# Where the operands of a chain of matmuls lie in SBUF, modulo 256 bytes

## The chip, the cores and the metric

The kernel runs on one core of one Trainium2 chip. The metric is the device time of one execution in microseconds (us), the median over several runs. Before the change it is 1124.74 us (three runs, 1123.02 to 1126.5).

## The reference

Four batches of twelve heads of attention over 448 positions (head size 64), with the scores capped by a tanh, feed two expert layers that all 1792 tokens go through:

```python
scores = cap * np.tanh(scale * np.matmul(q, k.transpose(0, 1, 3, 2)) / cap)
attn = softmax(scores)                                 # over the last axis
x = np.matmul(attn, v) ...                             # [1792, 768]
h = x @ w_in                                           # [768, 2048]
x = (h * np.cos(h)) @ w_out                            # [2048, 768]
a, b = x @ w1, x @ w2                                  # [768, 1024] each
out = ((a * b) @ w3) @ w_out2                          # [1024, 1024], [1024, 768]
```

The kernel computes w3 @ w_out2 first (called w2·w3 in what follows, after its tiles) and multiplies a * b by that product.

## The kernel before, in words

Every product is made of three matmuls in the type fp32r, since each operand is split into a high and a low part (tiles that end in h and l). The helper `mm3` issues them; its lines are 366, 367 and 368 of the profile:

```python
def mm3(out, wh, wl, xh, xl, first, last, on=False):
    PE.matmul(out, wh, xh, ...)   # L366: weights high, stream high
    PE.matmul(out, wh, xl, ...)   # L367: weights high, stream low
    PE.matmul(out, wl, xh, ...)   # L368: weights low, stream high
```

Each matmul loads its own 128x128 weights (a weight load, PEld) and then streams 448 columns (384 in w2·w3). So while L366 streams the high part, the weights of L367 are loaded; while L367 streams the low part, the weights of L368 are loaded; and while L368 streams the high part, the weights of the next L366 are loaded.

The program has four kinds of work. **Attention** (lines 577 to 605, 96 steps) streams the split queries qh, ql over the keys ks, and the probabilities p over v, in plain fp32 that takes several passes. Between its steps lie **w2·w3** (`make_w34`: stream w2, weights w3), and the start of **the first expert layer** (`moe1`: 384 calls of `mm3` with stream x and weights wi, 384 with stream g and weights wo). **The second expert layer** (`moe2`) is a Strassen-like scheme of seven products (`product`: 336 calls, stream y..., weights in the xh and xl tiles) followed by the output product (`o_unit`: 192 calls, stream ab, weights w34).

The order of all instructions is worked out when the kernel is built: each operation has a due time and a cost on each engine that may do it, and a planner (`Plan.schedule`) writes one list. On the chip each engine keeps that order and waits for the others through semaphores. The result of a unit of g is used by the matmuls two units later.

**Where the tiles lie.** `Ring` holds the buffers of one tile, `Pool` the pools. Pools of the left side begin where the one to the left ends; pools of the right side end at a fixed address and grow to the left. A tile lies behind the one created before it in its pool. A ring with `shift` gets 32 floats more and is read from `shift % PAD` floats on. `Ring.tile` gives the shifted view, `flat` the whole tile, and `seg` (L1087) cuts a segment of weights out of an x tile in the second expert layer. All chunks within a tile are multiples of 256 bytes apart where they are streamed, and of 512 where they are loaded as weights, so that each pair of tiles has one distance modulo 256. From the program before:

| stage | stream: address mod 256 | weights: address mod 256 |
|---|---|---|
| w2·w3 | w2h, w2l: 224 | w3h, w3l: 224 |
| first layer, into h | xh: 32, xl: 160 | wih, wil: 224 |
| first layer, out of g | gh, gl: 224 | woh, wol: 224 |
| second layer, products | y...h, y...l: 32 (yA22l: 160) | segments of xh: 96, of xl: 224 |
| second layer, output | abh: 32, abl: 160 | w34h, w34l: 224 |
| attention, scores | qh: 32, ql: 32 or 64 | ks: chunks at 32, 224, 160, 96 |

Of the kernel before, what the change touches and what calls it, by code (L numbers as in the profile page):

```python
# [10 lines left out]
F32 = mybir.dt.float32  # L11
F32R = mybir.dt.float32r
# [6 lines left out]
P = 128  # L19
B, H, S, D = 4, 12, 448, 64  # L20
CP = 112
NC = S // CP
DM = H * D
KD = DM // P
F1 = 2048
NF1 = F1 // P
F2 = 1024
# [5 lines left out]
INV2PI = 1.0 / (2.0 * math.pi)  # L33
CAP_MAX = 40.0
TWOPI = 6.283185
PAD = 32

# [3 lines left out]
class Ref:  # L43
    def __init__(self, item, sub=None, pick=None):
        self.item, self.sub, self.pick = item, sub, pick
# [25 lines left out]
class Ring:  # L71
# [7 lines left out]
    def tile(self, k):  # L79
        if not self.shift:  # L80
            return self.flat(k)
        t, n = self.flat(k), math.prod(self.shape[1:])
        t = t[:, self.shift % PAD:self.shift % PAD + n]
        return t if len(self.shape) == 2 else t.rearrange("p (a b) -> p a b", a=self.shape[1])

    def flat(self, k):
        if k not in self.tiles:
# [11 lines left out]


class Pool:
    def __init__(self, tc, name, **kw):
        self.tc, self.name, self.kw, self.rings, self.users = tc, name, kw, [], []

    def open(self):
        self.stack = ExitStack()
        self.pool = self.stack.enter_context(self.tc.tile_pool(name=self.name, bufs=1, **self.kw))

    def close(self):
        self.stack.close()  # L110


# [204 lines left out]
def program(  # L317
# [12 lines left out]
    general=False,  # L330
# [3 lines left out]
    G = dict(PAR, **GENERAL) if general else PAR  # L334
    plan = Plan()
# [38 lines left out]
    pools = {}  # L374

    def pool(name, **kw):
        pools[name] = Pool(tc, name, **kw)
        return pools[name]

    right = dict(side="right", reuse_waits="tile")  # L380
# [3 lines left out]
        pool(name, **kw)  # L384

    def ring(p, tag, shape, dtype=F32, n=2, shift=0):
        return Ring(plan, pools[p], tag, shape, dtype, n, shift)

    class Banks(Ring):
        def __init__(self, slots):  # L390
            Ring.__init__(self, plan, pools["psum"], "bank", [P, 512], F32, 0)
            self.free = [(0.0, k) for k in slots]
# [69 lines left out]
    ACT.activation(warm, warm, AF.Tanh)  # L462


    xh_r = ring("xring", "xh", [P, KD, S], F32R, 2, 0 if general else PAD)
    xl_r = ring("xring", "xl", [P, KD, S], F32R, 2, 0 if general else PAD)
    xh, xl = {}, {}
    A = {}
    tiles = [
# [380 lines left out]
    def pair(r):  # L850
        return r[0].ref(), r[1].ref()

    def hl(p, tag, shape, n, shift=0):
        return [ring(p, tag + t, shape, F32R, n, shift) for t in "hl"]
# [4 lines left out]
    def make_w34():  # L859

        raw_r, x_r = ring("wp", "raw", [P, 2 * DM], U32, G["nraw"]), ring("wp", "x", [P, DM], F32, G["nx"])
        w3_r = hl("wp", "w3", [P, F2 // 2], G["w3bufs"])
        w2_r = hl("wp", "w2", [P, DM], G["w2bufs"])
        sum_r = ring("wp", "sum", [P, DM], F32, NF2)
        NJ = NF2 // 2
        sums = [sum_r.new() for _ in range(NF2)]
        wo = {}
        runs = [(fc, p) for p in range(2) for fc in range(NF2)]
        need = {}
        for k, (fc, p) in enumerate(runs):  # L870
            need[fc, p] = G["wb"][p] + (G["we"][p] - G["wb"][p]) * fc / NF2
        for k, (fc, p) in enumerate(runs):
            due = need[fc, p]
            jcs = list(range(p * NJ, (p + 1) * NJ))

            new = {0: jcs, 3: [NJ], 6: [NJ + 1], NF2: jcs[2:]}.get(k, [])
            w3 = pair(w3_r)
            f64(due - G["e3"] * (k == 0), raw_r, x_r, w3T[fc, :, p * F2:(p + 1) * F2], F2 // 2, *w3)
            for n, jc in enumerate(new):
                wo[jc] = pair(w2_r)  # L880
                f64(due - (G["e2"] - n * G["e1"]) * (k == 0), raw_r, x_r, w_out2[jc], DM, *wo[jc])
            for n in range(2):
                half = slice(n * (DM // 2), (n + 1) * (DM // 2))
                acc = hy_r.ref()
                for q, jc in enumerate(jcs):
                    def f(acc=acc, q=q, jc=jc, half=half, w3=w3):
                        j = slice(q * P, (q + 1) * P)
                        mm3(acc()[:, :DM // 2], w3[0]()[:, j], w3[1]()[:, j], wo[jc][0]()[:, half],
                            wo[jc][1]()[:, half], q == 0, q == NJ - 1)

                    plan.op(due + n * 4 + q, [("PE", 3 * (DM / 4800 + 0.017), f)], r=[*w3, *wo[jc]], w=[acc])
                o = Ref(sums[fc], n, lambda t, half=half: t[:, half])
                a = acc[:, :DM // 2]
                if p == 0:
                    copy(due + n * 4 + 5, o, a, DM // 2, "AD", psum=True)
                else:
                    tt(due + n * 4 + 5, o, a, o, DM // 2, ALU.add, psum=True)
            if p == 1:
                z = w34_d.at(fc, lambda d, fc=fc: d[fc])
                o = Ref(sums[fc])  # L900
                dma(due + 12, z, o, r=[o], w=[z], kb=393, write=True)
        return raw_r, x_r
# [5 lines left out]
    def moe1(raw_r, x_r):  # L908
# [2 lines left out]
        wo_r = hl("mp", "wo", [P, DM], 4)  # L911
        hs_r, w_r = (ring("mp", t, [P, 2, S], F32, 2) for t in ("hs", "w"))
        kk_r = ring("mp", "kk", [P, S], F32, 1)
        g_r = hl("mp", "g", [P, 2, S], 2)
        y_r = ring("yp", "y", [P, KD, S], F32, 2)
        w_t, g_t, yacc = {}, {}, {}

# [26 lines left out]
        def chain(u, c, hp, due):  # L944

            if c == 0:
                g_t[u] = hs_r.new(), w_r.new()
            hs, w = (z.at(c, lambda t: t[:, c, :]) for z in g_t[u])
            copy(due, hs, hp, S, "AD", psum=True)
            plan.op(due + 1, [  # L950
                ("POOL", 0.16 + S / 1200,
                 lambda: POOL.tensor_scalar(w(), hs(), INV2PI, 0.25, op0=ALU.mult, op1=ALU.add)),
                ("DVE", 0.068 + S / 1920,
                 lambda: DVE.tensor_scalar(w(), hs(), INV2PI, 0.25, op0=ALU.mult, op1=ALU.add), True),
            ], r=[hs], w=[w])
            kk = kk_r.ref()
            plan.op(due + 2, [
                ("DVE", 0.068 + S / 1920,
                 lambda: DVE.tensor_scalar(kk(), w(), MAGIC, MAGIC, op0=ALU.add, op1=ALU.subtract), True),
            ], r=[w], w=[kk])  # L960
            tt(due + 3, w, w, kk, S, ALU.subtract, "PD")
            if c == 1:
                h2, w2 = (Ref(z) for z in g_t[u])
                plan.op(due + 5, [("ACT", 0.094 + 2 * S / 1200, lambda: ACT.activation(w2(), w2(), AF.Sin, scale=TWOPI))],  # L964
                        r=[w2], w=[w2], table="sin")
                tt(due + 6, w2, w2, h2, 2 * S, ALU.mult, "DP")
                g_t[u] = pair(g_r)
                copy(due + 7, g_t[u][0], w2, 2 * S, "APD")
                lo(due + 8, g_t[u][1], w2, g_t[u][0], 2 * S)

# [67 lines left out]
    def moe2():  # L1038
        raws = [ring("lp", "rawl", [P, 2 * DM], U32, 1), ring("q2", "rawq", [P, 2 * DM], U32, 1)]
        sts = [ring("lp", "stl", [P, DM], F32, 4), ring("q2", "stq", [P, DM], F32, 2)]  # L1040
        left_r = {x: hl("q2" if x == "A22" else "lp", f"y{x}", [P, KH, S], 1, PAD // 2 * (x == "A22")) for x in LEFT}
        w34_r, ab_r = hl("q2", "w34", [P, DM], 3), hl("q2", "ab", [P, S], 3, PAD // 2)
        c_r, tmp_r, ob_r = (ring("q2", t, [P, S], F32, n) for t, n in (("c", 11), ("tmp", 6), ("ob", 5)))
        V0, AB, OU = unit_due(4 * NP) + G["pu"], 63 * MM, 18 * MM
        left, right, cs = {}, {}, {}
# [39 lines left out]
                to("S4", a12, t + 5)  # L1085

        def seg(z, i, n):  # L1087
            if general:
                return z.tile().rearrange("p k s -> p (k s)")[:, i * HALF:(i + n) * HALF]
            return z.ring.flat(z.slot)[:, PAD // 2 + i * HALF:PAD // 2 + (i + n) * HALF]  # L1090

        def rights(p, fc, due):

# [79 lines left out]

        def o_unit(b, fc, due):

            w, ab = pair(w34_r), pair(ab_r)
            f32(due, sts[1], w34_d.at(fc, lambda d: d[fc]), DM, *w)
            halves(due - 1.5, ab, cs[b, fc], S)

            def one(m):  # L1180
                def go(at):
                    if fc == 0:
                        acc[m] = hy_r.ref()
                    o = acc[m]

                    def f():
                        mm3(o()[:, :S], w[0]()[:, m * P:(m + 1) * P], w[1]()[:, m * P:(m + 1) * P], ab[0](), ab[1](),
                            fc == 0, fc == NF2 - 1)

                    plan.op(at, [("PE", 3 * MM, f)], r=[*w, *ab], w=[o])  # L1190
                    if fc == NF2 - 1:
                        ob = ob_r.ref()
                        copy(at + 0.6, ob, o[:, :S], S, "AD" if m % 2 else "DA", psum=True)
                        dma(at + 1.5, Ref(out_i, (b, m)).view(lambda _: outT[b, m]), ob,
                            r=[ob], w=[Ref(out_i, (b, m))], kb=230, write=True)

                return go

            return [one(m) for m in range(KD)]
# [74 lines left out]
```

## Time and profile before

| | |
|---|---|
| median of three runs | 1124.74 us |
| time of the profiled execution | 1126.89 us |
| its span, first to last instruction | 1125.1 us |
| TensorE busy, matmuls (PE) | 1091.6 us, 97% |
| weight loads (PEld) | 941.1 us, 84% |
| VectorE (DVE) | 889.7 us, 79% |
| ScalarE (ACT) | 498.6 us, 44% |
| GpSimd (POOL) | 153.3 us, 14% |

PE is busy from the start of a matmul to its modelled end, and consecutive matmuls overlap; its busy share says that there was always one under way, not that the array ran at its peak. The weight loads run beside the matmuls. "L366" is a line of the kernel; helpers such as `mm3`, the copies (L342, L343) and the subtractions that make the low halves (L352) are called from many places, so the names of the tiles tell the stage.

### The profile page before, as it was taken

The numbers are of one execution on the slowest core, as the hardware profiler recorded it, in microseconds if no ns is written. First come the engines' busy times: TensorE is split into PE (matmuls) and PEld (weight loads), VectorE is DVE, ScalarE is ACT, GpSimd is POOL, SyncE is SP. The second block draws the span as 40 slices with busy tenths as digits, with TensorE's granted clock in tenths as the row PEclk, the third lists the DMA queues.
The fourth block names the chain that finished last, engine by engine and source line by source line (L and its number), as shares of the span: only waits on it lengthen the run. The fifth ranks groups of instructions, "written<-read, shape, count | busy, mean of one in ns | idle before, by whom it ended". The sixth has DMA issues, their size and how long they took to land. (4 is left out here: it accounts for less than half of the span.)

```text
span 1125.1 us, 13995 instructions
## 1 busy us (share of the span) xinstructions
PE 1091.6 (97%) x5040; PEld 941.1 (84%) x5040; DVE 889.7 (79%) x1353; ACT 498.6 (44%) x656; POOL 153.3 (14%) x145
## 2 busy tenths in 40 slices
PE   5899999999999999999999999999899999999997
PEld 3677777778888888889999999898789998999996
DVE  6888677799998989868789877777699879767642
ACT  4787667777655656541253211111244334221121
POOL 2222111112231111101001000000122200100000
PEclk9999999999999999999999999999899999999999
DMA  8885766877755655417633411104455435421132
GB/s 231 215 226 156 206 195 169 235 209 233 223 150 169 189 153 174 155 55 230 217 114 109 141 43 56 57 15 147 158 184 195 157 113 187 159 84 57 57 106 80
DMA packets 95554, 169.04 MB, mean 150 GB/s; under 512 B 37362, under 2 KB 68850, under 8 KB 95474
## 3 DMA queue, kind: packets, MB, share of 16 engines
q1 hardware_dynamic: 95474, 168.05, 49.7%
q8 instruction: 41, 0.67, 0.3%
q14 instruction: 39, 0.32, 0.1%
HBM read 129.30 MB, written 38.62 MB: 149 GB/s over the span
## 5 line engine op out<-in xcount | busy, mean ns | idle before, releaser
L605 PE MATMUL bank<-p,v 112*128 112x448 f32 x384 | 161.0, 542 | 0.0
L594 ACT ACTIVATE double<-double,ts 112x896 f32<-112x896 f32 x96 | 94.1, 981 | 76.9 <-PE double L585 76.7
L366 PE MATMUL bank<-xh,wih 128*128 128x448 f32 x270 | 108.3, 401 | 0.8 <-DVE xh L343 0.8
L605 PEld LDWEIGHTS bank<-p,v 112*128 112x128 f32 x384 | 72.8, 191 | 40.9 <-issue 38.0
L366 PE MATMUL bank<-gh,woh 128*128 128x448 f32 x260 | 102.3, 393 | 1.0 <-ACT hs L342 1.0
L367 PE MATMUL bank<-xl,wih 128*128 128x448 f32 x270 | 98.6, 365 | 0.2 <-DVE xl L352 0.2
L368 PE MATMUL bank<-xh,wil 128*128 128x448 f32 x270 | 98.4, 365 | 0.0
L594 ACT ACTIVATE p<-double,pac 112x896 f32<-112x896 f32 x96 | 96.9, 1011 | 2.4 <-PE bank L605 0.4
L367 PE MATMUL bank<-gl,woh 128*128 128x448 f32 x260 | 95.3, 367 | 0.0
L368 PE MATMUL bank<-gh,wol 128*128 128x448 f32 x260 | 95.1, 366 | 0.0
L352 DVE TENSOR_TENSOR y<-bank,y 128x448 f32<-128x448 f32 x111 | 68.5, 617 | 24.4 <-PE bank L368 24.0
L584 PE MATMUL double<-qh,ks 128*112 128x448 f32 x192 | 73.1, 381 | 13.7 <-DVE ks L352 9.7
L585 PE MATMUL double<-ql,ks 128*112 128x448 f32 x192 | 71.9, 375 | 0.0
L366 PEld LDWEIGHTS bank<-xh,wih 128*128 128x128 f32 x270 | 50.7, 188 | 10.2 <-issue 5.2
L366 PE MATMUL bank<-w2h,w3h 128*128 128x384 f32 x128 | 57.6, 450 | 1.7 <-ACT sum L342 1.7
L367 PEld LDWEIGHTS bank<-xl,wih 128*128 128x128 f32 x270 | 50.9, 188 | 9.3 <-issue 5.2
L819 POOL TENSOR_SCALAR wx<-rawc 128x768 f32<-128x768 f32 x29 | 34.7, 1195 | 168.0 <-DVE wil L352 65.8
L342 ACT COPY hs<-bank 128x448 f32<-128x448 f32 x39 | 20.8, 533 | 80.9 <-PE bank L368 80.9
L366 PEld LDWEIGHTS bank<-gh,woh 128*128 128x128 f32 x260 | 48.9, 188 | 8.7 <-issue 2.8
L367 PEld LDWEIGHTS bank<-gl,woh 128*128 128x128 f32 x260 | 49.0, 188 | 7.2 <-issue 3.5
L368 PEld LDWEIGHTS bank<-xh,wil 128*128 128x128 f32 x270 | 50.7, 188 | 3.9
L964 ACT ACTIVATE w<-w 128x896 f32<-128x896 f32 x32 | 30.5, 954 | 50.5 <-DVE w L352 50.4
(286 smaller groups left out, 2842.3 us busy)
## 6 DMA issues: line engine op xcount, KB each, us to landing
rawc<-in_w_out SPq DMA_DIRECT2D x16, 768.0 KB, 5.9
stq<-w_d SPq DMA_DIRECT2D x32, 384.0 KB, 3.4
qr<-in_q SPq DMA_DIRECT2D x48, 224.0 KB, 4.5
kr<-in_k SPq DMA_DIRECT2D x48, 224.0 KB, 4.8
rawc<-in_w_in SPq DMA_DIRECT2D x13, 768.0 KB, 4.9
raw<-in_w3T SPq DMA_DIRECT2D x16, 512.0 KB, 5.8
rawl<-in_w SPq DMA_DIRECT2D x9, 768.0 KB, 4.6
raw<-in_w_out SPq DMA_DIRECT2D x8, 768.0 KB, 6.9
```

The costliest lines, as they stand in the source:

```text
L342: "A": ("ACT", (0.051 if psum else 0.094) + n / 1200, lambda: ACT.copy(dst(), src())),
L352: "D": ("DVE", 0.068 + n / 960, lambda: DVE.tensor_tensor(dst(), a(), b(), op=op))
L366: PE.matmul(out, wh, xh, start=first, stop=False, skip_group_check=on)
L367: PE.matmul(out, wh, xl, start=False, stop=False, skip_group_check=on)
L368: PE.matmul(out, wl, xh, start=False, stop=last, skip_group_check=on)
L584: PE.matmul(o, w, qh(), start=True, stop=False)
L585: PE.matmul(o, w, ql(), start=False, stop=True)
L594: lambda f=f, x=x, o=o: ACT.activation(o(), s(), f, scale=x[:CP]))],
L605: PE.matmul(pv()[:, :S], w()[:, 2 * c + n].rearrange("p a d -> p (a d)"), p()[:, n, :], start=c == 0 and n == 0, stop=c == NT - 1 and n == 1)
L819: lambda: POOL.tensor_scalar(x(), h_().bitcast(F32), 0.0, 1.0, op0=ALU.mult, op1=ALU.mult)),
L964: plan.op(due + 5, [("ACT", 0.094 + 2 * S / 1200, lambda: ACT.activation(w2(), w2(), AF.Sin, scale=TWOPI))], r=[w2], w=[w2], table="sin")
```

## The change: addresses only

No instruction is added, removed or moved in the program; operands lie elsewhere. The padding of a shifted ring becomes 64 floats (256 bytes), and its view starts at `shift` floats (16 floats are 64 bytes, 48 are 192). The x rings lose their padding. w3 gets a shift of 48 floats; g becomes one tile with both halves and a shift of 16; ab becomes one tile with both halves and a shift of 16; yA22 keeps 16. The pool lp gets 16 floats at its front and the pool q2 gets 48 floats at its back. The weights' segments are now read from the start of the x tiles.

```diff
-PAD = 32
+PAD = 64
+PADS = {("lp", "front"): 16, ("q2", "back"): 48}
...
-        t = t[:, self.shift % PAD:self.shift % PAD + n]
-        return t if len(self.shape) == 2 else t.rearrange("p (a b) -> p a b", a=self.shape[1])
+        t = t[:, self.shift:self.shift + n]
...
+    def pad(self, end):
+        n = self.pads.get((self.name, end))
+        if n:
+            self.pool.tile([P, n], F32, name=f"{end}_{self.name}", bufs=1)
...
     def open(self):
...
+        self.pad("front")
 
     def close(self):
+        self.pad("back")
         self.stack.close()
...
-    xh_r = ring("xring", "xh", [P, KD, S], F32R, 2, 0 if general else PAD)
-    xl_r = ring("xring", "xl", [P, KD, S], F32R, 2, 0 if general else PAD)
+    xh_r = ring("xring", "xh", [P, KD, S], F32R, 2)
+    xl_r = ring("xring", "xl", [P, KD, S], F32R, 2)
...
-        w3_r = hl("wp", "w3", [P, F2 // 2], G["w3bufs"])
+        w3_r = hl("wp", "w3", [P, F2 // 2], G["w3bufs"], 48)
...
-        g_r = hl("mp", "g", [P, 2, S], 2)
+        g_r = ring("mp", "g", [P, 2, 2, S], F32R, 2, 16)
...
-                g_t[u] = pair(g_r)
+                g = g_r.new()
+                g_t[u] = [g.at(n, lambda t, n=n: t[:, n]) for n in range(2)]
...
-        left_r = {x: hl(..., [P, KH, S], 1, PAD // 2 * (x == "A22")) for x in LEFT}
-        w34_r, ab_r = hl("q2", "w34", [P, DM], 3), hl("q2", "ab", [P, S], 3, PAD // 2)
+        left_r = {x: hl(..., [P, KH, S], 1, 16 * (x == "A22")) for x in LEFT}
+        w34_r, ab_r = hl("q2", "w34", [P, DM], 3), ring("q2", "ab", [P, 2, S], F32R, 3, 16)
...
-            return z.ring.flat(z.slot)[:, PAD // 2 + i * HALF:PAD // 2 + (i + n) * HALF]
+            return z.tile().rearrange("p k s -> p (k s)")[:, i * HALF:(i + n) * HALF]
```

## Rows read from the trace of the kernel before

**Rows 1.** The page's part 1: busy us, share of the span, instructions

```profile
PE 1091.6 (97%) x5040; PEld 941.1 (84%) x5040; DVE 889.7 (79%) x1353; ACT 498.6 (44%) x656; POOL 153.3 (14%) x145
```

**Rows 2.** Busy time by stretch: PE, PEld, DVE, ACT, POOL; then clock, DMA share, GB/s

```profile
560.00:660.00 100.00, 100.00 (x491) 91.97 (x490) 89.38 (x147) 35.93 (x57) 10.35 (x9) 1.00 0.37 116
...
800.00:960.00 160.00, 153.09 (x735) 139.55 (x735) 144.36 (x224) 64.54 (x102) 22.33 (x16) 0.98 0.53 175
960.00:1125.10 165.10, 156.85 (x773) 144.60 (x772) 95.61 (x152) 32.58 (x55) 6.21 (x7) 0.99 0.27 85
```

**Rows 3.** What PE waited for: us in total, times, longest

```profile
PE bank L366 <- DVE yA22h L343: 2.8, 1, 2.8
PE bank L368 <- DVE w34l L352: 1.7, 1, 1.7
```

**Rows 4.** Timeline of PE in the first layer: start us, us, instruction

```profile
601.53 0.37 PE L366 MATMUL bank<-xh,wih 128*128 128x448 f32 x1
...
602.74 0.36 PE L366 MATMUL double<-gh,woh 128*128 128x448 f32 x1
...
603.97 0.36 PE L366 MATMUL bank<-xh,wih 128*128 128x448 f32 x1
```

**Rows 5.** Timeline of all engines near the end: a weight load beside a matmul

```profile
1115.19 0.36 PE L367 MATMUL bank<-abl,w34h 128*128 128x448 f32 x1
1115.19 0.19 PEld L368 LDWEIGHTS bank<-abh,w34l 128*128 128x128 f32 x1
```

**Rows 6.** Groups of PE in 500 to 795 us: count, busy us, mean ns

```profile
L366 PE MATMUL bank<-gh,woh 128*128 128x448 f32 x122 | 44.8, 367 | 0.0
...
L367 PE MATMUL bank<-gl,woh 128*128 128x448 f32 x122 | 44.8, 367 | 0.0
L368 PE MATMUL bank<-gh,wol 128*128 128x448 f32 x122 | 44.7, 366 | 0.0
...
L368 PE MATMUL bank<-xh,wil 128*128 128x448 f32 x108 | 39.4, 365 | 0.0
L367 PE MATMUL bank<-xl,wih 128*128 128x448 f32 x108 | 39.4, 364 | 0.0
L366 PE MATMUL bank<-xh,wih 128*128 128x448 f32 x108 | 39.4, 364 | 0.0
```

**Rows 7.** The same of PE in 960 to 1125 us, the second layer

```profile
L367 PE MATMUL bank<-abl,w34h 128*128 128x448 f32 x48 | 17.5, 366 | 0.0
...
L366 PE MATMUL bank<-abh,w34h 128*128 128x448 f32 x48 | 17.3, 360 | 0.0
...
L368 PE MATMUL bank<-yS2h,xl 128*128 128x448 f32 x12 | 4.4, 367 | 0.0
...
L366 PE MATMUL bank<-yA22h,xh 128*128 128x448 f32 x12 | 4.4, 366 | 0.0
L367 PE MATMUL double<-yA22l,xh 128*128 128x448 f32 x12 | 4.4, 366 | 0.0
...
L367 PE MATMUL bank<-yS2l,xh 128*128 128x448 f32 x12 | 4.4, 363 | 0.0
...
L366 PE MATMUL bank<-yS2h,xh 128*128 128x448 f32 x11 | 4.0, 363 | 0.0
```

**Rows 8.** The same of PE in 60 to 180 us, w2·w3

```profile
L367 PE MATMUL bank<-w2l,w3h 128*128 128x384 f32 x91 | 30.6, 336 | 0.0
```

**Rows 9.** Timeline of PE in one attention step, scores

```profile
146.03 0.36 PE L584 MATMUL double<-qh,ks 128*112 128x448 f32 x1
146.23 0.37 PE L585 MATMUL double<-ql,ks 128*112 128x448 f32 x1
146.44 0.37 PE L584 MATMUL double<-qh,ks 128*112 128x448 f32 x1
146.65 0.36 PE L585 MATMUL double<-ql,ks 128*112 128x448 f32 x1
```

**Rows 10.** Timeline of DVE at the start of the second layer

```profile
797.11 0.63 DVE L352 TENSOR_TENSOR tmp<-bank,tmp 128x448 f32<-128x448 f32 x1 [3.94 <-PE bank L368]
...
802.46 0.38 DVE L343 CAST yA22h<-stq 128x448 fp32r<-128x448 f32 x1
```

More of the change, by code (lines that the diff above doesn't have):

```diff
@@ L82, in tile @@
         t, n = self.flat(k), math.prod(self.shape[1:])
-        t = t[:, self.shift % PAD:self.shift % PAD + n]
-        return t if len(self.shape) == 2 else t.rearrange("p (a b) -> p a b", a=self.shape[1])
+        t = t[:, self.shift:self.shift + n]
+        if len(self.shape) == 2:
+            return t
+        if len(self.shape) == 3:
+            return t.rearrange("p (a b) -> p a b", a=self.shape[1])
+        return t.rearrange("p (a b c) -> p a b c", a=self.shape[1], b=self.shape[2])
     def flat(self, k):
@@ L101, with __init__ @@
 class Pool:
-    def __init__(self, tc, name, **kw):
-        self.tc, self.name, self.kw, self.rings, self.users = tc, name, kw, [], []
+    def __init__(self, tc, name, pads, **kw):
+        self.tc, self.name, self.pads, self.kw, self.rings, self.users = tc, name, pads, kw, [], []
+    def pad(self, end):
+        n = self.pads.get((self.name, end))
+        if n:
+            self.pool.tile([P, n], F32, name=f"{end}_{self.name}", bufs=1)
     def open(self):
@@ L376, in pool @@
     def pool(name, **kw):
-        pools[name] = Pool(tc, name, **kw)
+        pools[name] = Pool(tc, name, {} if general else PADS, **kw)
         return pools[name]
@@ L386, in ring @@
     def ring(p, tag, shape, dtype=F32, n=2, shift=0):
-        return Ring(plan, pools[p], tag, shape, dtype, n, shift)
+        return Ring(plan, pools[p], tag, shape, dtype, n, 0 if general else shift)
     class Banks(Ring):
@@ L1040, in moe2 @@
         sts = [ring("lp", "stl", [P, DM], F32, 4), ring("q2", "stq", [P, DM], F32, 2)]
-        left_r = {x: hl("q2" if x == "A22" else "lp", f"y{x}", [P, KH, S], 1, PAD // 2 * (x == "A22")) for x in LEFT}
-        w34_r, ab_r = hl("q2", "w34", [P, DM], 3), hl("q2", "ab", [P, S], 3, PAD // 2)
+        left_r = {x: hl("q2" if x == "A22" else "lp", f"y{x}", [P, KH, S], 1, 16 * (x == "A22")) for x in LEFT}
+        w34_r, ab_r = hl("q2", "w34", [P, DM], 3), ring("q2", "ab", [P, 2, S], F32R, 3, 16)
         c_r, tmp_r, ob_r = (ring("q2", t, [P, S], F32, n) for t, n in (("c", 11), ("tmp", 6), ("ob", 5)))
@@ L1087, in seg @@
         def seg(z, i, n):
-            if general:
-                return z.tile().rearrange("p k s -> p (k s)")[:, i * HALF:(i + n) * HALF]
-            return z.ring.flat(z.slot)[:, PAD // 2 + i * HALF:PAD // 2 + (i + n) * HALF]
+            return z.tile().rearrange("p k s -> p (k s)")[:, i * HALF:(i + n) * HALF]
         def rights(p, fc, due):
@@ L1174, in o_unit @@
         def o_unit(b, fc, due):
-            w, ab = pair(w34_r), pair(ab_r)
+            w, ab = pair(w34_r), ab_r.new()
+            ab = [ab.at(n, lambda t, n=n: t[:, n]) for n in range(2)]
             f32(due, sts[1], w34_d.at(fc, lambda d: d[fc]), DM, *w)
```

## The prediction

> **What bounds the kernel now.** I read the page's busy times first, then the stretches, the waits of TensorE, the timeline of a steady stage, and last the groups of matmuls with their mean durations. Matmuls are under way for 1091.6 of the 1125.1 us span [rows 1], and in the first layer for 100.00 of 100 us [rows 2]. What TensorE waits for after the start is a few single events of 1 to 3 us [rows 3]. The clock is granted in full in the first layer (1.00, the 2.4 GHz level), so no clock hides behind the busy time. The kernel goes at the pace of the matmul chain: 491 matmuls in 100 us are 204 ns from start to start, where 448 columns at 2.4 GHz are 187. Some 17 ns per matmul are not streaming.
>
> Is that remainder the same everywhere? In the timeline six matmuls of stream x take 1.21 us (601.53 to 602.74), and the next six, of stream g, take 1.23 (602.74 to 603.97) [rows 4]. Their form is the same; the tiles differ. A matmul's row says 0.36 us though the next one starts 0.20 us later: the modelled end adds about 0.16 us to every row, so differences between mean durations are differences of pace, and I work with these. In the first layer stream g has 366 to 367 ns, stream x 364 to 365 [rows 6]; in the second, the rows go from 360 to 367 [rows 7].
>
> What differs is where the operands lie. The weight load of the next matmul starts together with the stream of the present one and lies beside it (both at 1115.19, 0.19 us of it) [rows 5]. So the pair that may collide is a stream and the *following* load. From the table of addresses, its distance (stream minus next weights, modulo 256) is 0 for all of g; 64 for xh, 192 for xl; for y it is 192 behind L366 and L368 and 64 behind L367; for yA22 192 throughout; for ab 64 behind abh within a unit and 192 behind abl. Beside the rows: distance 0 has 366 to 367; distance 64 has 364 and 365 (xh), 363 (yS2l), 360 (abh, L366); distance 192 has everything: 363 (yS2h, L366), 364 (xl), 366 (abl, yA22h, yA22l), 367 (yS2h, L368). So 64 is low each time in matmuls with 128 columns of weights, 0 is high, and 192 is mixed.
>
> **The change part by part.** Addresses after it, worked out from the order of the tiles. The x tiles are 42 times 256 bytes without padding, so xh and xl all lie at 32; wi stays at 224. Both g tiles grow by 256 bytes: g lies at 224 + 64 = 32, wo at 224. w3 lies at 224 + 192 = 160 and w2 at 224. lp begins 64 bytes behind 32, so y lies at 96, and its weights, now at the start of the x tiles, at 32. q2 grows by 192 more than a multiple of 256 and ends where it did, so w34 moves to 32, ab and yA22 to 96. Attention moves as a whole by a multiple of 256. Every stream and following load in the two layers and in w2·w3 is then 64 apart; attention keeps its distances.
>
> What each part is worth in duration of matmuls (negative is gain):
> - g: 1152 matmuls go from distance 0 to 64. They should do as x does, whose streams lie at 32 over weights at 224 exactly as g then will: 366.7 to 364.3 on the mean of three rows [rows 6], -2.4 ns each, -2.8 us.
> - Products of the second layer, L368 (336): 367 at 192 to the 363 to 364 of yS2l at 64 [rows 7]: -3.5 ns, -1.2 us. L366, at 363 already, is taken at nothing.
> - yA22, L366 and L367 (96): 366 to 363: -0.3 us.
> - ab, L367 (192): 366 to 363: -0.6 us.
> - xl, L367 (384): 364 at 192, at most 1 ns to gain: -0.2 us, between 0 and -0.4.
> - w2·w3 (384): distance 0, and no row shows this shape elsewhere. Its row has 336 [rows 8], which less the 0.16 us is some 175 ns against 160 of streaming. The bounds: -0.9 us by the gain of g, +3.8 us if it goes the way of the attention row below (10 ns). I take -0.6, nearer to g, since it is the same three-line helper with 128 columns of weights.
>
> Sum: -5.7 us. Part of it is not kept: from 800 to 960 us VectorE is busy for 144.36 of 160 us [rows 2], and there TensorE waits for a low half that VectorE makes (w34l, 1.7 us) [rows 3]. If TensorE comes earlier, this wait grows. The gain in that stretch is about 1.5 us; I give back 0.4. The largest wait, 2.8 us for yA22h at the start of the second layer [rows 3], does not grow: VectorE's row before that chain had itself waited 3.94 us for a matmul [rows 10], so the chain starts earlier with TensorE. Net -5.3 us.
>
> What costs nothing: merging g's two halves, and ab's, in one tile adds no instruction. Both halves are freed by the same last matmul before and after. If a reader of the high half had now to wait for the low half, the matmuls concerned come two units later for g, which covers the VectorE subtraction; without that cover it is one wait of at most 1 us per unit, 32 units. New neighbours in reused memory can only add a wait for tiles whose last reader is long done at that point of the order.
>
> The profiled execution took 1126.89 us, 1.8 beyond its span and 2.2 above the median of the runs. From it, -5.3 gives 1121.6; from the median of 1124.74, which the time is compared with, **1119.4 us**.
>
> The Trainium skill speaks against any gain: "TensorE: Matmul & The Clock Gate", section "Step-by-step: what each phase is for", says that TensorE has two independent SBUF read ports, so that loading the next weights takes no read bandwidth from the running matmul. By that rule the sum would be 0, which is the first rival below; the trace bears it out for the overlap as such [rows 5], but rows of one form that differ by 7 ns [rows 7] speak against it in full.
>
> **The rivals.**
> 1. *Distance is not the cause.* What differs between tiles may be their order in the chain (L368 precedes a change of weights, g follows attention) or the traffic of other engines. For it: xl at 192 is as fast as xh at 64 [rows 6], and the same 192 gives 363 and 367 [rows 7]. Against it: g and x alternate in the same stretch with the same neighbours, and the low rows are at 64 three times. The change then does little: 0 to -3.4 us, 1121.4 to 1124.7, 1123.5 in the middle. Chance 0.24.
> 2. *The pace falls further.* abh reaches 360 at 64 [rows 7]. If all 3888 matmuls of the two layers came near that, 3 to 4 ns each below the mean of about 364.5, it is -8 to -15 us: 1110 to 1116. Against it: xh at 64 has 364 to 365 in over 200 rows [rows 6]. Chance 0.09.
> 3. *64 is the worse distance where weights or streams change shape.* In attention qh streams while the same chunk of ks is loaded once more; at distance 0 (146.03) the next start comes after 0.20 us, at distance 64 (146.44) after 0.21 [rows 9]. The order of the distances is turned round there. If that holds for w2·w3 (up to +3.8 us), and for the L366 of the products and for xl, which leave 192 (672 matmuls, up to +3 ns, +2.0), while g gains little (-0.5), the time is about 1130. It decides from the point where these lose more than g gains. Against it: ks has 112 columns of weights, and its chunks are 448 bytes apart. Chance 0.06.
>
> **How the numbers follow.** The forecast has 0.61, with -3.4 to -8 us. The likeliest is 1119.4. The range of 8 in 10 goes from 1114.0, well into rival 2, to 1124.0, which takes in most of rival 1; it leaves out the far end of rival 2 and all of rival 3. What a measurement of this kernel can tell from no change is about 0.3%, 3.4 us. Faster by more: forecast and rival 2, 0.70. Within: rival 1, 0.24. Slower: rival 3, 0.06.
>
> **What would show it.** In the profile after, the rows of stream g should read 364 to 365 instead of 366 to 367, and L368 of the products 363 to 364 instead of 367; abl and yA22 near 363; attention's rows unchanged. w2·w3 should read some 334 to 335. The stretch of the first layer without attention should be about 1% shorter per matmul for g's half. VectorE's, ScalarE's and GpSimd's rows and counts should stay, and the waits of rows 3 stay within half a us. If g's rows stay at 366 to 367 at the new distance, rival 1 holds and the prediction is wrong at its first step; if they fall but the time does not, it is the waits.

## The result, and the profile after

| | before | after |
|---|---|---|
| median of the runs compared | 1126.37 us (6) | 1115.24 us (6) |
| ratio, 95% interval | | 0.9906 [0.9887, 0.9925] |
| span of the profiled execution | 1125.1 us | 1114.7 us |

The change makes the kernel 0.94% faster, 10.6 us by the ratio (8.4 to 12.7 by its interval); the forecast was 5.3 us. The order of the instructions is the same on every engine; ScalarE and GpSimd have one semaphore wait more each. The lines of the profile are 12 higher than before: L366 to L368 of `mm3` are L378 to L380, L343 is L355, L352 is L364.

The page's busy times of the kernel after, to be read against [rows 1]:

```profile
PE 1078.9 (97%) x5040; PEld 937.4 (84%) x5040; DVE 885.6 (79%) x1353; ACT 498.4 (45%) x656; POOL 156.1 (14%) x145
```

Matmuls are under way for 12.7 us less (1091.6 to 1078.9), the span is shorter by 10.4: TensorE's idle time has grown by 2.3 us in this execution. The stretches, columns as in [rows 2]:

```profile
555.00:655.00 100.00, 99.88 (x500) 93.16 (x499) 89.66 (x148) 35.98 (x57) 10.70 (x9) 1.00 0.37 120
795.00:955.00 160.00, 154.10 (x754) 141.55 (x755) 144.60 (x224) 64.38 (x102) 22.52 (x16) 0.99 0.55 181
955.00:1114.70 159.70, 151.16 (x754) 140.70 (x752) 92.19 (x146) 31.53 (x53) 6.20 (x7) 0.98 0.24 80
```

In 100 us of the first layer stand 500 matmuls, where there were 491. That is 200 ns from one to the next instead of 204, at the same clock. The timeline, columns as in [rows 4]:

```profile
594.33 0.36 PE L378 MATMUL bank<-xh,wih 128*128 128x448 f32 x1
...
595.52 0.36 PE L378 MATMUL double<-g,woh 128*128 128x448 f32 x1
...
596.73 0.36 PE L378 MATMUL bank<-xh,wih 128*128 128x448 f32 x1
...
597.92 0.36 PE L378 MATMUL double<-g,woh 128*128 128x448 f32 x1
...
599.12 0.36 PE L378 MATMUL bank<-xh,wih 128*128 128x448 f32 x1
...
600.33 0.36 PE L378 MATMUL double<-g,woh 128*128 128x448 f32 x1
```

Six matmuls of x take 1.19 us, six of g 1.21, then x 1.19, g 1.20 and x 1.21. Both are faster, and what is left between them is scatter of single sixes. The groups of the first layer, 495 to 787 us, as in [rows 6]:

```profile
L380 PE MATMUL bank<-g,wol 128*128 128x448 f32 x122 | 44.2, 362 | 0.0
...
L379 PE MATMUL bank<-g,woh 128*128 128x448 f32 x122 | 44.1, 362 | 0.0
L378 PE MATMUL bank<-g,woh 128*128 128x448 f32 x122 | 44.1, 361 | 0.0
...
L380 PE MATMUL bank<-xh,wil 128*128 128x448 f32 x108 | 39.1, 362 | 0.0
L379 PE MATMUL bank<-xl,wih 128*128 128x448 f32 x108 | 39.1, 362 | 0.0
L378 PE MATMUL bank<-xh,wih 128*128 128x448 f32 x108 | 39.0, 361 | 0.0
```

g fell from 366 to 367 down to 361 to 362, further than x stood before; and x itself fell from 364 to 365 to 361 to 362, in all three lines. The second layer, 955 to 1115 us, as in [rows 7]:

```profile
L379 PE MATMUL bank<-ab,w34h 128*128 128x448 f32 x48 | 17.4, 362 | 0.0
L378 PE MATMUL bank<-ab,w34h 128*128 128x448 f32 x48 | 17.3, 360 | 0.0
...
L379 PE MATMUL double<-yA22l,xh 128*128 128x448 f32 x12 | 4.3, 362 | 0.0
...
L380 PE MATMUL double<-yS2h,xl 128*128 128x448 f32 x12 | 4.3, 362 | 0.0
L378 PE MATMUL bank<-yA22h,xh 128*128 128x448 f32 x12 | 4.3, 361 | 0.0
...
L380 PE MATMUL bank<-yS2h,xl 128*128 128x448 f32 x9 | 3.3, 363 | 0.0
L379 PE MATMUL bank<-yS2l,xh 128*128 128x448 f32 x9 | 3.3, 362 | 0.0
L378 PE MATMUL bank<-yS2h,xh 128*128 128x448 f32 x9 | 3.2, 360 | 0.0
```

Every row of [rows 6] and [rows 7] that stood at 366 or 367 is at 360 to 363. L366 of the products, forecast to stay at 363, came down to 360 as well. What TensorE waits for, as in [rows 3]:

```profile
PE bank L378 <- DVE yA22h L355: 2.8, 1, 2.8
PE bank L378 <- DVE xh L355: 2.2, 1, 2.2
PE bank L380 <- DVE w34l L364: 1.7, 1, 1.7
```

The two waits of [rows 3] are as long as they were. New in this size is the one for xh. In the timelines of TensorE, of the kernel before and then of the one after, it stands here:

```profile
223.89 0.37 PE L368 MATMUL bank<-xh,wil 128*128 128x448 f32 x1
225.06 0.47 PE L366 MATMUL bank<-xh,wih 128*128 128x448 f32 x1 [0.80 <-DVE xh L343]
```

```profile
221.32 0.36 PE L380 MATMUL bank<-xh,wil 128*128 128x448 f32 x1
223.91 0.49 PE L378 MATMUL bank<-xh,wih 128*128 128x448 f32 x1 [2.23 <-DVE xh L355]
```

TensorE arrives 2.57 us earlier, but leaves only 1.15 us earlier: VectorE, which makes xh there, is not on TensorE's pace. This is one execution: the profile of `abs0` below, whose matmuls go at the same pace, has no such wait.

### The profile page after: what moved, and what is told of

The parts are those of the page before. It is cut to its first block, busy times and chain, and to the rows that moved or that the text cites. A ratio compares the mean times of both kernels' runs of the same rounds, so it can differ in the third digit from the quotient of the medians.

```text
span 1114.7 us, 13997 instructions
## 1 busy us (share of the span) xinstructions
PE 1078.9 (97%) x5040; PEld 937.4 (84%) x5040; DVE 885.6 (79%) x1353; ACT 498.4 (45%) x656; POOL 156.1 (14%) x145
## 5 line engine op out<-in xcount | busy, mean ns | idle before, releaser
L378 PE MATMUL bank<-xh,wih 128*128 128x448 f32 x270 | 107.8, 399 | 2.7 <-DVE xh L355 2.2
L378 PE MATMUL bank<-g,woh 128*128 128x448 f32 x260 | 100.7, 387 | 0.0
L380 PE MATMUL bank<-xh,wil 128*128 128x448 f32 x270 | 98.0, 363 | 0.0
L380 PE MATMUL bank<-g,wol 128*128 128x448 f32 x260 | 94.2, 362 | 0.0
L379 PE MATMUL bank<-g,woh 128*128 128x448 f32 x260 | 94.1, 362 | 0.0
L364 DVE TENSOR_TENSOR y<-bank,y 128x448 f32<-128x448 f32 x111 | 68.5, 617 | 21.8 <-PE bank L380 21.3
L378 PEld LDWEIGHTS bank<-xh,wih 128*128 128x128 f32 x270 | 50.7, 188 | 11.7 <-issue 5.0
L378 PE MATMUL bank<-w2h,w3h 128*128 128x384 f32 x128 | 57.5, 449 | 0.0
L379 PEld LDWEIGHTS bank<-g,woh 128*128 128x128 f32 x260 | 48.8, 188 | 6.7 <-issue 3.5
L378 PEld LDWEIGHTS bank<-g,woh 128*128 128x128 f32 x260 | 48.8, 188 | 6.6 <-issue 2.8
L380 PEld LDWEIGHTS bank<-xh,wil 128*128 128x128 f32 x270 | 50.8, 188 | 3.4
```

The source lines that it names most:

```text
L364: "D": ("DVE", 0.068 + n / 960, lambda: DVE.tensor_tensor(dst(), a(), b(), op=op))
L378: PE.matmul(out, wh, xh, start=first, stop=False, skip_group_check=on)
L379: PE.matmul(out, wh, xl, start=False, stop=False, skip_group_check=on)
L380: PE.matmul(out, wl, xh, start=False, stop=last, skip_group_check=on)
```

## The experiments

A measure that needs less rounding than the rows: the mean time from the start of a matmul to the start of the next, from the start times of the trace, without matmuls next to attention's fp32 ones and without gaps over 230 ns. In what follows, g, x and so on "have" such a time. Before, g has 204.6 ns, x 202.4, products 202.7, yA22 203.7, ab 201.5 and w2·w3 174.9. After, all five streams of 448 columns have 200.0 to 200.1, w2·w3 173.3. Each comes from one profiled execution. Ratios of times are against the kernel before on the same chip.

**One part alone, and from the other side.** `g_alone` puts g 64 bytes further within its pool by two spacers, in the kernel before:

```diff
+SPACE = {("gh", 0): 16, ("woh", 2): 48}     # floats before that tile
...
+            n = self.plan_space.get((self.tag, k))
+            if n:
+                self.pool.pool.tile([P, n], F32, name=f"space_{self.tag}{k}", bufs=1)
```

> The kernel before with the first layer's g alone moved 64 bytes behind wo (g at 32, wo at 224 modulo 256; g stays two tiles, nothing else moves). Distance theory: g's rows fall from 366 to 367 ns to 361 to 362, and time by 1152 matmuls of about 4.5 ns, 5 us. The x rows stay at 364 to 365 if a matmul's pace hangs on its own distance alone; they fall to near 362 if x gained after the change because g, its neighbour in the stage, moved. If the gain came from merging g's halves in one tile or from the other moves: g's rows stay at 366 to 367, time within 1 us of before.

Time 0.9977 [0.9965, 0.9989]. Its groups in 500 to 785 us (L373 to L375 are `mm3`):

```profile
L374 PE MATMUL bank<-gl,woh 128*128 128x448 f32 x122 | 44.4, 364 | 0.0
L375 PE MATMUL bank<-gh,wol 128*128 128x448 f32 x122 | 44.2, 363 | 0.0
L373 PE MATMUL bank<-gh,woh 128*128 128x448 f32 x122 | 44.1, 361 | 0.0
L374 PE MATMUL bank<-xl,wih 128*128 128x448 f32 x108 | 39.6, 367 | 0.0
...
L373 PE MATMUL bank<-xh,wih 128*128 128x448 f32 x108 | 39.1, 362 | 0.0
```

g goes to 200.6 ns without being merged into one tile. The mean of x stays at 202.4, but is dealt out anew among its lines: L366 is 2 ns faster, L367 3 ns slower. A single line's row is therefore no measure of that line's distance; the mean over the three is. The time fell by 2.6 us, under the 4.6 that the pace gives; the ends of the interval are 1.2 and 3.9. No run shows where the rest went.

`wo_moved` has 16 floats more at the back of the pool, so g is back at 224 and wo at 160:

```diff
+SPACE = {("gh", 0): 16, ("woh", 2): 48}
+BACK = {"mp": 16}
```

> The same distance of 64 made from the other side: g stays at 224 modulo 256 and its weights wo move to 160. Distance theory: g's L366 and L367 fall to 361 to 362 ns as in the run with g moved; L368 before a load of wi (distance 0 there) keeps some of its loss; x before a load of wo is now at 128. Time 3 to 5 us under before. Theory that the absolute address of the stream counts (224 slow, 32 fast): g's rows stay at 366 to 367, time within 1 us of before.

g has 200.6 ns again, x 201.7, where `g_alone` left it at 202.4; the time is 0.9958 [0.9945, 0.9972]. Moving the weights does for g what moving the stream does: the distance counts, and not the stream's own address. L368 of g, which was expected to keep some of its loss, is the fastest of the three lines, 198.6 ns.

`x_alone` reads xl from 128 bytes further on:

```diff
-        t = t[:, self.shift % PAD:self.shift % PAD + n]
+        off = PAD if self.tag == "xl" else self.shift % PAD
+        t = t[:, off:off + n]
```

> The kernel before with xl alone read from 128 bytes further on in the first layer, so that it lies 64 and not 192 bytes behind the weights that are loaded beside it; xh, g and the second layer stay. In the profile after the change x gained 2.5 ns in all three lines though xh had kept its distance. If a matmul's pace hangs on the distances of its neighbours too (L367 at 64 helps L366 and L368): all three x lines fall from 364 to 365 to near 362, time by 1152 matmuls of 2 ns, 2.3 us. If each matmul counts by itself: L367 falls by at most 1 to 2 ns, L366 and L368 stay, time by 0.4 to 0.8 us. If x gained from g's move: nothing falls here.

x comes to 201.2 ns (200.9, 202.2 and 200.5 in its three lines, from 202.4, 202.6 and 202.3), g to 203.7; time 0.9983 [0.9973, 0.9993]. So L366 and L368, whose distances did not change, gained 1.5 and 1.8, and L367, whose distance did, 0.4. A matmul's pace hangs on its neighbours' distances too.

`first_layer` has both edits, g and xl.

> The kernel before with both edits of the first layer, g at 64 and xl at 64; second layer and w2w3 as before. Alone, g came to 600.6/3 = 200.6 ns with x unmoved at 202.4, and xl's move brought x to 201.2 with g near its old pace (203.7). If the two stages, which alternate every six matmuls, help each other: both near 200.1 as in the changed kernel, time 0.65% under before (2304 matmuls of 3.3 ns, 7.6 us), more than the two runs alone (0.23 and 0.17%) add up to. If they merely add: g 200.6 and x 201.2, time 0.45% under before. The second layer's rows must stay at those of before.

g has 200.2 and x 200.1 ns; in the second layer the products have 202.8 and ab 201.4, as before. The time is 0.9937 [0.9913, 0.9960]. Alone, g gained 4.0 ns, which left x where it was, and x 1.2, with 0.9 for g beside it; together they gain 4.4 and 2.3. A part of the gain of x comes only when both move. In time that is 7.1 us against 2.6 and 1.9 for the parts, with intervals of 1 to 3 us on each.

**The distance swept.** In the changed kernel all distances are set to one value by the paddings; here for 32, the others alike:

```diff
-PADS = {("lp", "front"): 16, ("q2", "back"): 48}
+PADS = {("xring", "front"): 56, ("lp", "front"): 8, ("q2", "back"): 48}
...                                     # w3: shift 56, g and ab: 8, yA22: 0
```

> The changed kernel with every distance set to 0 instead of 64 in both layers and w2w3 (only the paddings differ). Distance theory: all rows of both layers read 366 to 368 ns, as g did before, w2w3 336; 3888 matmuls of 5 ns and 384 of 2 make the time 20 us longer than the changed kernel, about 1136, so some 9 us longer than before. If the gain is in the new tiles or paddings and not in the distance, the time stays near 1115.

> The changed kernel with every distance 32 in place of 64. If 64 sits in the middle of a good stretch of distances, 32 lies on its edge: a pace between 200.1 ns (all at 64) and 203 to 204 (all at 0), some 201.5, time 1120. If only 0 is bad (the two accesses coincide): 200 ns and 1115 to 1116. If 64 alone is good: 203 and 1126.

> The changed kernel with every distance 96. Good stretch around 64: about 201.5 ns, time 1120, like 32. Only 0 is bad: 200 ns, 1115. 64 alone is good: 203 ns, 1126.

> The changed kernel with every distance 128. Good stretch around 64: 203 ns, time 1126, as at 0. Only 0 is bad: 200 ns, 1115. The kernel before has this distance only in attention's scores, where its rows were neither the fastest nor the slowest.

> The changed kernel with every distance 192, which in the kernel before gave fast rows (yS2h in L366) and slow ones (yS2h in L368, yA22). If the mean over the three lines of a helper call is what the distance sets: 203 to 204 ns in all of them, as yA22 had (203.7 with all three at 192), time 1126 to 1128. If each line counts by itself: L366 201 to 202, L368 206, the mean again near 203. Only 0 is bad: 200 ns, 1115.

| distance | time against before, 95% | g, x | products | ab | w2·w3 |
|---|---|---|---|---|---|
| 0 | 1.0004 [0.9987, 1.0020] | 202.7, 202.8 | 204.1 | 203.5 | 175.9 |
| 32 | 1.0051 [1.0034, 1.0068] | 205.2, 205.2 | 205.8 | 203.8 | 175.4 |
| 64 (the change) | 0.9906 [0.9887, 0.9925] | 200.1, 200.1 | 200.1 | 200.0 | 173.3 |
| 96 | 1.0056 [1.0042, 1.0070] | 205.3, 205.3 | 205.1 | 205.0 | 176.5 |
| 128 | 1.0002 [0.9988, 1.0016] | 203.9, 203.8 | 203.8 | 203.3 | 176.2 |
| 192 | 0.9967 [0.9950, 0.9984] | 202.2, 202.2 | 202.6 | 201.7 | 174.8 |

The verdict stands in the stretch 560 to 660 us of each, columns as in [rows 2]; the count behind the busy time of PE is what to read, here of the kernels with 0, 32 and 192:

```profile
560.00:660.00 100.00, 99.97 (x494) 92.29 (x493) 89.59 (x147) 35.85 (x57) 10.46 (x9) 1.00 0.37 116
```

```profile
560.00:660.00 100.00, 100.00 (x485) 90.76 (x484) 88.31 (x145) 35.97 (x57) 10.04 (x9) 1.00 0.36 113
```

```profile
560.00:660.00 100.00, 99.95 (x495) 92.28 (x494) 88.68 (x146) 34.73 (x55) 9.31 (x9) 1.00 0.36 114
```

494, 485 and 495 matmuls, where 64 has 500. All five streams follow the distance, so the distance theory stands in its main point. They are within 0.1 ns of each other at 64, but up to 2.0 apart elsewhere (203.8 for ab and 205.8 for the products at 32). Its shape was expected wrongly. 0 does not cost 20 us more than 64 but some 11 (1.0004 against 0.9906 of 1126 us), and is not the worst; 64 is not the middle of a good stretch, since 32 and 96 on either side of it are the worst values tried; and 192 is second best, where 203 to 204 was expected.

Why 0 costs less than expected stands in the table: g has 202.7 ns where everything is at 0, but had 204.6 in the kernel before, at the same distance beside an x at 64 and 192. The expectation had taken a pace from a mixed stage for that of a distance.

**How narrow, and is it the distance alone?** `near64` has g at 80 and ab at 48 (shifts 20 and 12 in place of 16).

> The changed kernel with g at distance 80 and ab at 48; the rest stays at 64. If the distance must be a multiple of 64 (32 and 96 gave 205.2): g and ab at 203 to 205 ns, time 3 to 7 us over the changed kernel. If there is a narrow valley around 64: 201 to 203. x, which alternates with g, may rise by up to 1 ns.

g 202.4, ab 202.6, x 201.0 ns, time 0.9953 [0.9941, 0.9965]: 16 bytes off costs more than half of what g had gained, and ab all of its 1.5 and more. x loses 0.9 beside g; the products, which alternate with ab, keep 200.1.

`abs0` moves streams and weights together by 32 bytes:

```diff
-PADS = {("lp", "front"): 16, ("q2", "back"): 48}
+PADS = {("xring", "front"): 56, ("lp", "front"): 16, ("wi", "back"): 8, ("q2", "back"): 56}
```

> The changed kernel with all streams and weights of the layers and w2w3 moved together by 32 bytes (streams at 0 or 64 modulo 256, weights at 192 or 0), distances kept at 64. If the distance alone counts: 200 ns, time within 0.2% of the changed kernel, 1115. If the position in a line of 64 bytes counts as well (until now all weights and most streams lay 32 bytes into one): the pace moves by some ns, faster or slower than 200.

x and the products have 200.1 ns, g 200.2, ab 200.0; the time is 0.9895 [0.9872, 0.9919], not to be told from the changed kernel. At this distance and for this shift, where a stream begins does not count beside how far it is from the weights.

`wil_near` puts wil alone at 32, by laying the three wih tiles first, a spacer of 16 floats, then the wil tiles.

> The changed kernel with wil alone moved by 64 bytes (the high weights wih stay). In L367 xl then streams at distance 0 to the weights loaded beside it (wil) and 64 to its own (wih); in L368 xh streams at 64 to the next load and at 0 to its own weights. If the load beside the stream counts: x in L367 slows from 200 to about 203 ns, L368 stays, in all 1 to 2 us more. If the stream's distance to its own weights counts: L368 slows and L367 stays. g's rows stay at 200 to 201.

Time 0.9922 [0.9898, 0.9947]. Its groups of x in 500 to 785 us:

```profile
L380 PE MATMUL bank<-xh,wil 128*128 128x448 f32 x106 | 38.6, 365 | 0.0
L379 PE MATMUL bank<-xl,wih 128*128 128x448 f32 x106 | 38.6, 364 | 0.0
L378 PE MATMUL bank<-xh,wih 128*128 128x448 f32 x106 | 38.4, 362 | 0.0
```

x rises to 201.3 ns, in L367 by 1.5 and in L368 by 1.3; g, which was expected to stay, rises to 200.8. Inconclusive: since losses are dealt out among the lines of a call, this doesn't tell the load beside a stream from its own weights. Two other numbers pull opposite ways. In `wo_moved` the last stream before the other stage lies beside a load at 0 (g) or 128 (x), yet the mean of the two stages is no worse, 201.2 ns against 201.5 in `g_alone`: as if the distance to its own weights counted. In the kernel before, yA22 lies at 192 to its own weights in one line of three, but to the load beside it in nearly all, and has 203.7 ns: as if the load counted.

## Why the prediction was right, and what was mis-sized

The cause that was forecast is the one the runs show: part for part, pace follows the distance between stream and weights modulo 256. The size is not. The forecast's own band was -3.4 to -8 us; 10.6 us lies beyond it, in the 8 to 15 us of rival 2 (the pace falls further), which had a chance of 0.09. The time of 1115.24 us is in the range of 1114.0 to 1124.0 because that range was drawn well into rival 2; for the forecast's own sum this is luck.

Rival 2 came true in its size: the mean over the 3888 matmuls of the two layers fell by 3.0 ns, from 203.0 to 200.1. Not all rows came to its 360; they read 360 to 363. What was held against it, xh at 364 to 365 though at 64, fails for the reason given below. Rival 1 (distance is not the cause) is refuted by `g_alone`, `wo_moved` and the sweep. Rival 3 (64 is the worse distance where shapes change) was wrong for w2·w3, which gained 1.6 ns on the mean of its lines (its L367, the row of [rows 8], reads 336 before and after). Its ground was attention's rows at 64 [rows 9], and over all of them the kernel before agrees: qh over ks has 201.1 ns at distance 0 (44 matmuls) and 204.8 at 64 (46). After the change, at the same distances, they have 202.3 and 202.2, and the mean of all scores moved between 202.4 and 203.4 in the kernels run here, though no distance in them changed. Attention alternates four distances from chunk to chunk, so these rows measure no single one. What one distance throughout would give there was not tried.

The forecast was half of what was measured. Term by term, from the mean pace (ns) times the matmuls:

| term | forecast | measured |
|---|---|---|
| g | -2.8 us | 4.5 x 1152 = -5.2 us |
| x | -0.2 us | 2.3 x 1152 = -2.6 us |
| products without yA22 | -1.0 us of the 1.2 | 2.6 x 864 = -2.2 us |
| yA22, all three lines | -0.3 and 0.2 us of the 1.2 | 3.7 x 144 = -0.5 us |
| ab | -0.6 us | 1.5 x 576 = -0.9 us |
| w2·w3 | -0.6 us | 1.6 x 384 = -0.6 us |
| given back in waits | +0.4 us | +2.3 us here, +0.7 in `abs0` |

The sum without waits is -12.0 us, where -5.7 was forecast; the busy time fell by 12.7. The step that was mis-sized stands in the prediction's first bullet: g "should do as x does, whose streams lie at 32 over weights at 224 exactly as g then will". x as measured before was not at 64 throughout. Its L367 stood at 192, and it alternated with g at 0. `x_alone` shows that the 192 held x back by 1.2 ns, `first_layer` that g at 0 held it back by another 1.1. The second does not come by itself: in `g_alone`, with xl still at 192, x gained nothing. The yardstick moved together with what was measured by it. For the same reason "at most 1 ns to gain" for xl was wrong: only the line whose distance changed was counted, and the gain came in the lines beside it. L366 of the products, "at 363 already ... taken at nothing", gained 3.1 ns in the same way.

The term for waits was expected where VectorE is busiest, at w34l. The longer of the two waits there stayed at 1.7 us; the shorter grew, here before, after and in `abs0`:

```profile
PE double L368 <- DVE w34l L352: 1.1, 1, 1.1
```

```profile
PE double L380 <- DVE w34l L364: 1.5, 1, 1.5
```

```profile
PE double L380 <- DVE w34l L364: 1.3, 1, 1.3
```

That is 0.4 and 0.2 us more; 0.4 was forecast. Most of the 2.3 us by which TensorE's idle time grew is the wait for xh at 221 us, 1.4 us longer than before. It is not shown to come with the change: `abs0` goes at the same pace without it, and there the idle time is 34.2 us (a span of 1113.4 less the busy time below), only 0.7 more than before.

```profile
PE 1079.2 (97%) x5040; PEld 938.6 (84%) x5040; DVE 885.9 (80%) x1353; ACT 498.7 (45%) x656; POOL 153.9 (14%) x145
```

The Trainium skill says in "TensorE: Matmul & The Clock Gate", section "Step-by-step: what each phase is for", that loading the next weights takes no read bandwidth from the running matmul. From that alone no gain followed, yet the same matmuls beside the same loads took 200.0 to 205.8 ns as the addresses alone changed. Whether the load takes bandwidth after all or something else makes the difference stays open; no run shows it. Also open is whether the load beside a stream or the stream's own weights count.

## What to carry to other kernels

If a chain of matmuls that each load their own weights bounds the time, compare the mean durations of rows of one shape. Where they differ by a few ns, look at the distance modulo 256 bytes between a stream and the weights loaded beside it; here 64 was best and 32 or 96 worst, 1.5% of the time apart. Lay out all the stages that alternate, since one at a poor distance can slow its neighbours (x by 0.9 ns beside g at 80, though the products not at all beside ab at 48), and don't take as the target pace the rows of a stage that has such neighbours. Expect a part back as waits where another engine keeps its own time; here it was 0.7 to 2.3 of 12 us, in two executions.

## What the runs showed of the hardware that was not expected

- From one execution each: among distances of 0, 32, 64, 96, 128 and 192 bytes modulo 256 the order was 64 (200.1 ns), 192 (202.2), 0 (202.7), 128 (203.8), 32 and 96 (205.2), in the first layer. That the odd multiples of 64 do best, the even ones worse and the odd multiples of 32 worst was not foreseen. 64 and 192 lead in every stage; the order of the rest differs. 160 and 224 weren't tried.
- A distance counts modulo 256 and not modulo 512: in the kernel after, the streams of x and g at 64 and those at 320 modulo 512 have the same pace line for line, within 0.2 ns. Nor is 128 the period, since 64 and 192 differ by 2.1.
- Sixteen bytes off 64 cost 2.3 ns of g's 4.5 (distance 80), and 2.6 for ab (48), which had gained 1.5.
- Losses are dealt out among the three lines of a call: with g at 64 and x untouched, xl's rows went from 364 [rows 6] to 367 and xh's L366 from 364 to 362, at the same mean for x.
- At 64, a matmul of 448 columns takes 26.8 ns more than one of 384 (200.1 and 173.3), 0.42 ns a column, which is one cycle of the granted 2.4 GHz. By that 448 columns are 187 ns, and even at the best distance 13 ns per matmul are left over. No stream of the two layers went below a mean of 200.0 over its lines in any run here.
